# Block-sparse attention with a feed-forward layer: transposing P of the first 28 pairs on the tensor engine, and starting the feed-forward layer at slot 16

## The chip, the cores and the metric

The kernel runs on one core of a Trainium2 chip. The metric is device time in microseconds (us); lower is better. A core has a tensor engine (PE), a vector engine (DVE), a scalar engine (ACT), a GpSimd engine (POOL) and a sync engine (SP), each with its own in-order queue of instructions, and 16 DMA engines that all queues share.

## The reference

Attention over 4 batches, 8 heads, 768 positions, head size 64, with a mask by blocks of 32 positions: a block of queries sees its own block and its neighbours, the first and the last block, and three sampled blocks; the first and last query blocks see everything. Behind it stand a layer norm, a feed-forward layer (512 to 2048 to 512, ReLU) and a residual sum.

```python
scores = where(mask, q @ k.T / sqrt(D), -1e9)
attn   = softmax(scores)                    # per head, 768 x 768, block-sparse
x      = (attn @ v) -> (B, S, H * D)        # 4 x 768 x 512
xn     = (x - mean) / sqrt(var + 1e-6) * g_ln
out    = x + relu(xn @ w_ch1) @ w_ch2
```

Nearly every product is made of fp16 halves (a high part and a low part of each operand), so one product takes two or three matmuls.

## The kernel before

**Tiles, slots and pairs.** The rows of the output are 24 tiles of 128 query rows (two batches by two query blocks). 22 are sparse tiles with 8 x 32 keys each (kind "s"), and two, the 12th and the last, are dense ones ("d"). A tile has 8 heads; one head of one tile is a *slot*, so there are 192 slots, 0 to 191. In sparse tiles two heads are a *pair* (slots 2n and 2n+1 are pair n, until slot 87); softmax and the transpose of P are done once for a pair.

**The main loop** runs over slots `i`; for PE, SP and POOL its order is the program's order, while the order on DVE and ACT is set by the framework's scheduler. In slot `i` come, in this order: loads that an agenda has put there; the scores of slot `i` (16 matmuls in `scores`, tile `ps`, line 407, or 393 in a dense tile); after a pair's second slot its softmax (`softmax`: DVE takes the minimum, ACT makes exp into `e`, ACT casts the high half of `p`, DVE makes the low half, line 448); one slot later the transpose of `p` into `pt` (`transposes`, a DMA transpose of 256 KB issued by SP, line 459); and the product with V of slot `i - LAG`, LAG = 6 (`attn_v`, 16 matmuls into `pa`, line 481). After a tile's last head its layer norm follows (`layer_norm`), and when both tiles of a group of two have been normed, two slots later, their transposes (`ln_transposes`, 16 transposes on PE into `px`, line 516, two copies by ACT into `xT`, line 517).

**The feed-forward layer** (`ffn`) is a generator per group. It is stepped NFF = 24 times a slot from slot FF0 = 27 on. A slot's 24 steps are 24 up-projection matmuls of 256 columns (`pu`, line 533), whose 512 results per row ACT turns into `hh` (line 541) and DVE into `hl` (line 542); or 12 down-projection matmuls of 512 columns (`po`, line 552; each takes two steps). A group takes 8 slots of the first kind and 8 of the second, and a new group comes every 16 slots, so the layer keeps its distance behind the attention to the end. Behind each tile's down-projection stands the residual sum on DVE (line 558) and the store of `out`, issued by SP at once (line 560).

**Buffers.** `pu`, `po` and `px` take turns in one pool of three PSUM buffers (`ps_f`). `p` and `e` have two buffers each, `pt` three, the group's `xT`, `hh` and `hl` one each.

**Weights and K, V.** The weights come as 64-bit floats and are converted on the chip while attention runs: w1 in 8 pieces around slots 2 to 16, w2 in 16 pieces at slots 18 to 33 (a load on SP, three DVE operations, lines 224 to 228, ACT operations, lines 200 and 201 or 217 and 218, and a subtraction on POOL, line 203 or 220). K and V of the first two batches are split into halves before slot 0 and written to DRAM (`krow`, `vrow`; `write_k`, `first_v`, issued by SP); those of the other two from slot 50 on (`load_k`, slots 50 to 55; `load_v`, slots 57 to 62). A tile's K and V are read from there by SP (`kg`, `vg`) and gathered by POOL.

Of the kernel before, what the change touches and what calls it, by code (L numbers as in the profile page):

```python
# [44 lines left out]
def sparse_attention_moe(  # L45
# [26 lines left out]
    FF0 = 27  # L72
# [179 lines left out]
    def first_k(kr):  # L252
        kh, kl = (x[:, 0 : NB * H * BLK].rearrange("p (k e) -> p k e", k=NB) for x in k_f)
        for j in range(6):
# [4 lines left out]
            if j % 2:  # L259
                write_k(0, slice(4 * j - 4, 4 * j + 4), (kh, kl), slice(4 * j - 4, 4 * j + 4),  # L260
                        nc.sync)

    def first_v(vr):
        for b in range(2):
            for t in range(6):
# [4 lines left out]
                nc.sync.dma_start(vrow[0][t * P : (t + 1) * P, b, :],  # L270
                                  vs.rearrange("p h d -> p (h d)"))

    def write_k(f, bl, halves, src, dma):
# [236 lines left out]
    def ln_transposes(gr):  # L510
        gr.xT = lnp.tile([P, 2, CT, 2 * P], F16, tag="xT", name=f"xT{gr.i}")
        for j, t in enumerate(gr.tiles):
# [4 lines left out]
            nc.scalar.copy(gr.xT[:, :, :, j * P : (j + 1) * P], pt)  # L517


    def ffn(gr):  # L520
        N = 2 * P
        hh = hp.tile([P, FT, N], F16, tag="hh", name=f"hh{gr.i}")
        hl = hp.tile([P, FT, N], F16, tag="hl", name=f"hl{gr.i}")
        for f in range(0, FT, 2):
            ph = ps_f.tile([P, 512], F32, tag="pf", name=f"pu{gr.i}_{f}")
            while (1, f // 2) not in ready:
                yield
            for j in range(2):
                fs = slice((f + j) * P, (f + j + 1) * P)
                n = 0  # L530
                for w, i in ((w1h, 0), (w1l, 0), (w1h, 1)):
                    for ct in range(CT):
                        nc.tensor.matmul(ph[:, j * N : (j + 1) * N], w[:, ct, fs],  # L533
                                         gr.xT[:, i, ct, :], start=n == 0, stop=n == 3 * CT - 1,
                                         skip_group_check=True)
                        n += 1
                        if j == 0 or n < 3 * CT:
                            yield
            dh = hh[:, f : f + 2, :].rearrange("p f n -> p (f n)")
            dl = hl[:, f : f + 2, :].rearrange("p f n -> p (f n)")  # L540
# [208 lines left out]
```

## Time and profile before

| | |
|---|---|
| time, median of 3 runs | 905.37 us (904.17 to 906.74) |
| time of the profiled execution | 909.08 us |
| its span, first to last instruction | 907.2 us |
| mean granted clock of PE over the span | 0.906 of full speed |
| PE busy | 683.1 us (75%) |
| DVE busy | 466.8 us (51%) |
| ACT busy | 385.8 us (43%) |
| POOL busy | 314.3 us (35%) |

The profiled execution took 3.71 us more than the median, and 1.88 us of its time lie outside the span. A share of busy time is a mean over stages with different limits: PE is nearly always busy in the second half and mostly idle in the first quarter. So the views by stretch say more than this table.

### The profile page before, as it was taken

The page shows a single profiled execution, that of the slowest core. Times are in us where ns is not written, and L with a number is a line of the kernel's source. Part 1 is how long each engine was busy: PE and PEld are TensorE (multiplying, and loading weights), DVE is VectorE, ACT ScalarE, POOL GpSimd, SP SyncE. Part 2 cuts the span into 40 slices and gives each one's busy share as a digit, 9 for nine tenths or more (in the row PEclk, how much of TensorE's full clock was granted, in tenths as well). Part 3 has the DMA queues.
Part 4 walks back from the last instruction along what each step waited for, and adds up shares of the span by engine and source line. Part 5 has one row for each costly group of instructions (what it writes and reads, how often), then busy time and mean ns, then how long its engine had stood idle before and what let it go on. Part 6 is the DMA issues. An engine that isn't in the chain of part 4 may idle for free.

```text
span 907.2 us, 24132 instructions
## 1 busy us (share of the span) xinstructions
PE 683.1 (75%) x10304; PEld 446.9 (49%) x10304; DVE 466.8 (51%) x1144; ACT 385.8 (43%) x867; POOL 314.3 (35%) x284
## 2 busy tenths in 40 slices
PE   0011131548996767799987799999999999998998
PEld 0011121335583455366565376575856758466583
DVE  3638397577456443355573354455655546564120
ACT  3435364344454555344463244454444445543120
POOL 1247346435446766530060433343432331000000
PEclk9999555678998887799998799999999999999999
DMA  9999985939986979978999987878967697777000
GB/s 347 311 306 250 258 208 138 257 96 253 219 200 154 267 207 243 194 190 172 196 207 222 200 188 166 188 187 198 164 155 170 168 221 167 178 126 150 12 13 24
DMA packets 209226, 171.72 MB, mean 189 GB/s; under 512 B 151136, under 2 KB 176352, under 8 KB 208736
## 3 DMA queue, kind: packets, MB, share of 16 engines
q1 hardware_dynamic: 194064, 129.00, 61.5%
q0 software_dynamic: 13376, 40.91, 17.8%
q8 instruction: 81, 1.33, 0.7%
q10 hardware_dynamic: 1680, 0.28, 0.2%
q14 instruction: 25, 0.20, 0.1%
HBM read 121.91 MB, written 18.87 MB: 155 GB/s over the span
## 4 chain that ended last, share of the span: by engine, by line
PE 43%; DMA 26%; DVE 12%; ACT 8%; SPq 5%; issue 5%; POOL 0%; ACTq 0%; DVEq 0%; POOLq 0%
PE po L552 19%; PE pu L533 17%; DMA pt<-p 10%; DMA qr<-qT 7%; DMA vg<-vrow 3%; PE ps L407 3%; DVE p L448 3%; ACT e L443 3%; PE pa L481 3%; SPq L459 2%; ACT p L447 2%; DMA kr<-kT 2%; DVE e L436 2%; DVE st L440 1%; DVE hl L542 1%
## 5 line engine op out<-in xcount | busy, mean ns | idle before, releaser
L533 PE MATMUL pu<-xT,w1h 128*128 128x256 f16 x1536 | 224.8, 282 | 0.0
L481 PE MATMUL pa<-vg,pt 128*32 128x64 f16 (+1 forms) x3584 | 79.5, 217 | 133.4 <-DMA pt<-p 106.2
L340 POOL DMA_INDIRECT kg<-krow,ik x132 | 133.5, 1011 | 112.5 <-PE pa L481 42.4
L533 PEld LDWEIGHTS <-w1h 128*128 128x128 f16 x1536 | 148.0, 101 | 27.8
L448 DVE SCALAR_TENSOR_TENSOR p<-e,p 128x512 f16<-128x512 f32 (+1 forms) x104 | 92.6, 891 | 128.4 <-ACT p L447 128.1
L443 ACT ACTIVATE e<-e,st 128x256 f32<-128x256 f32 (+1 forms) x192 | 102.8, 536 | 126.1 <-DVE st L440 106.3
L552 PE MATMUL po<-w2h,hh 128*128 128x512 f16 x384 | 150.2, 391 | 0.4 <-DVE x L558 0.4
L552 PE MATMUL po<-w2l,hh 128*128 128x512 f16 x384 | 149.2, 389 | 0.0
L552 PE MATMUL po<-w2h,hl 128*128 128x512 f16 x384 | 149.1, 388 | 0.0
L313 POOL TENSOR_TENSOR ql<-qr,qx 64x1024 f16<-64x1024 f32 x24 | 51.0, 2124 | 236.8 <-ACT qx L312 236.7
L481 PEld LDWEIGHTS <-pt 128*32 128x32 f16 x3584 | 60.4, 102 | 141.9 <-DMA pt<-p 110.0
L533 PE MATMUL pu<-xT,w1l 128*128 128x256 f16 x768 | 121.6, 283 | 0.0
L552 PEld LDWEIGHTS <-hh 128*128 128x128 f16 x768 | 70.3, 100 | 81.2 <-issue 7.3
L436 DVE CUSTOM_DVE_ANT_1 e<-ps,bias 128x256 f32<-128x256 f32 x176 | 67.3, 418 | 67.4 <-PE ps L407 64.5
L407 PE MATMUL ps<-kg,qx 128*32 128x96 f16 (+1 forms) x1408 | 56.2, 236 | 52.1 <-DMA kg<-krow 44.7
L541 ACT ACTIVATE hh<-pu 128x512 f16<-128x512 f32 x96 | 56.4, 591 | 80.7 <-PE pu L533 80.3
L447 ACT CAST p<-e 128x512 f16<-128x512 f32 (+1 forms) x104 | 67.6, 650 | 53.2 <-DMA pt<-p 51.1
L533 PEld LDWEIGHTS <-w1l 128*128 128x128 f16 x768 | 78.1, 102 | 11.6
L542 DVE SCALAR_TENSOR_TENSOR hl<-pu,hh 128x512 f16<-128x512 f32 x96 | 65.8, 685 | 34.3 <-ACT hh L541 33.9
L407 PEld LDWEIGHTS <-qx 128*32 128x32 f16 x1408 | 25.1, 101 | 100.5 <-issue 98.6
L552 PEld LDWEIGHTS <-hl 128*128 128x128 f16 x384 | 38.4, 100 | 47.8 <-issue 4.1
L357 POOL DMA_INDIRECT vg<-vrow,iv x44 | 42.4, 963 | 47.4 <-PE pa L481 28.3
(82 smaller groups left out, 728.3 us busy)
## 6 DMA issues: line engine op xcount, KB each, us to landing
vg<-vrow SPq DMA_DIRECT2D x44, 384.0 KB, 6.3
qr<-qT SPq DMA_DIRECT2D x24, 512.0 KB, 8.2
kg<-krow SPq DMA_DIRECT2D x22, 512.0 KB, 6.9
w2r<-w SPq DMA_DIRECT2D x16, 512.0 KB, 5.7
out<-x SPq DMA_DIRECT2D x24, 256.0 KB, 3.0
kg<-krow SPq DMA_DIRECT2D x8, 768.0 KB, 9.9
vg<-vrow SPq DMA_DIRECT2D x8, 768.0 KB, 7.4
w2l<-w SPq DMA_DIRECT2D x4, 1024.0 KB
```

The source lines that it names most:

```text
L313: nc.gpsimd.tensor_sub(t.ql[0:D], qr[0:D], t.qx[0:D])
L340: nc.gpsimd.indirect_dma_start(t.k[:, 4 * j + 5 + r].rearrange("p b e -> p (b e)"), None, krow[t.f].rearrange("k p b e -> (k p) (b e)"), b ...
L407: nc.tensor.matmul(dst, q[:, h, rows], rhs, start=n == 0 and k == 0 and h % 2 == 0, stop=n == 1, skip_group_check=True)
L436: nc.vector.tensor_tensor_reduce(out=pr.e[:, k].rearrange("p (b k) -> p b k", k=BLK), in0=pr.ps[:, k], in1=bb, scale=-0.125, scalar=3.0e38 ...
L443: nc.scalar.activation(pr.e[:, k], pr.e[:, k], AF.Exp, bias=st[:, 1, h0 + k : h0 + k + 1], scale=-1.0, accum_out=st[:, 2, h0 + k : h0 + k ...
L447: nc.scalar.copy(pr.p[:, 0], e)
L448: nc.vector.scalar_tensor_tensor(out=pr.p[:, 1], in0=e, scalar=1.0, in1=pr.p[:, 0], op0=ALU.mult, op1=ALU.subtract)
L481: nc.tensor.matmul(t.xa[rows, h % 4, 0:w], pr.pT[:, i, k0 + k, rows], vv[:, k, 0:w], start=first and k == 0 and i == 0, stop=k == nk - 1 a ...
L533: nc.tensor.matmul(ph[:, j * N : (j + 1) * N], w[:, ct, fs], gr.xT[:, i, ct, :], start=n == 0, stop=n == 3 * CT - 1, skip_group_check=True)
L541: nc.scalar.activation(dh, ph, AF.Relu)
L542: nc.vector.scalar_tensor_tensor(out=dl, in0=ph, scalar=0.0, in1=dh, op0=ALU.max, op1=ALU.subtract)
L552: nc.tensor.matmul(po, x[:, f, ts], w[:, f, :], start=f == 0 and n == 0, stop=f == FT - 1 and n == 2)
```

## The change

Seven edits go together.

1. P of pairs 0 to 27 (slots 0 to 55) is no longer transposed by a DMA. `pe_transposes` does it in slot 2n + 4 for pair n (PELAG = 3 slots behind the pair's second slot): 8 transposes of 128 columns on PE into a buffer `pp` of the pool of three, and one copy of 128 x 1024 by ACT into `pt`. Pairs from 28 on keep the DMA transpose.
2. FF0 goes from 27 to 16. (NFF0 is 24 like NFF, so the steps per slot stay.)
3. The first group's layer-norm transposes are done tile by tile, two slots behind each tile's norm, that is in slots 15 and 23.
4. The first group's up-projection runs twice over the 8 pieces of w1, once per tile, with 128 columns instead of 256: slots 16 to 23 and 24 to 31. Its down-projection then takes slots 32 to 39, and group g (from 1 on) starts in slot 16g + 24 instead of 16g + 27.
5. The store of an output tile is issued at the start of a slot two slots behind the residual sum, not right behind it.
6. The high half of the first K is written to DRAM by ACT's queue and the low half by SP's.
7. The first V's 12 writes go to ACT's queue.

```diff
-    FF0 = 27
+    FF0 = 16
+    NFF0, FF0END = 24, 44
+    PEP, PELAG = 28, 3
...
                 write_k(0, slice(4 * j - 4, 4 * j + 4), (kh, kl), slice(4 * j - 4, 4 * j + 4),
-                        nc.sync)
+                        (nc.scalar, nc.sync))
...
-                nc.sync.dma_start(vrow[0][t * P : (t + 1) * P, b, :],
-                                  vs.rearrange("p h d -> p (h d)"))
+                nc.scalar.dma_start(vrow[0][t * P : (t + 1) * P, b, :],
+                                    vs.rearrange("p h d -> p (h d)"))
...
+    def pe_transposes(pr):
+        k = len(pr.heads) * 2
+        pr.pT = ptp.tile([P, 2, k, P], F16, tag="pt", name=f"pt{pr.i}")
+        pt = ps_f.tile([P, 2 * k, P], F16, tag="pf", name=f"pp{pr.i}")
+        p = pr.p.rearrange("p i k -> p (i k)")
+        for c in range(2 * k):
+            nc.tensor.transpose(pt[:, c], p[:, c * P : (c + 1) * P], ident)
+        nc.scalar.copy(pr.pT.rearrange("p i k q -> p (i k) q"), pt)
...
+        for lo, hi in ((0, 1), (1, 2)) if gr.i == 0 else ((0, 2),):
+            cs = slice(lo * P, hi * P)
+            N = (hi - lo) * P
+            for f in range(0, FT, 2):
+                ph = ps_f.tile([P, 512], F32, tag="pf", name=f"pu{gr.i}_{lo}_{f}")
+                while (1, f // 2) not in ready or gr.have < hi:
+                    yield
...
-            nc.sync.dma_start(out[t.i], x)
+            outq.append([2, t.i, x])
...
+            for o in outq:
+                o[0] -= 1
+            while outq and outq[0][0] <= 0:
+                _, n, x = outq.pop(0)
+                nc.sync.dma_start(out[n], x)
...
-                transposes(slots[i - 1].pr)
+                if slots[i - 1].pr.i >= PEP:
+                    transposes(slots[i - 1].pr)
+            if 0 <= i - PELAG < NS:
+                pr = slots[i - PELAG].pr
+                if pr.i < PEP and slots[i - PELAG] is pr.slots[-1]:
+                    pe_transposes(pr)
...
-                    if s.t.i % 2:
-                        lnq.append((i + 2, gr))
+                    if gr.i == 0:
+                        lnq.append((i + 2, gr, (s.t.i,)))
+                    elif s.t.i % 2:
+                        lnq.append((i + 2, gr, (0, 1)))
```

What it moves on the queues, at three places. First SP's queue between the start-up and slot 9, before (`vrow` are writes of the first V, `w2l` and `w2h` here loads of raw w1, `pt` transposes of P, `vg` loads of V):

```order
L350 DMA vg0_128<-vrow0_136 96x2048 x2
L270 DMA vrow0_136<-vs0_1_5_252 128x1024
L191 DMA w2l_125<-w1 128x4x512
L311 DMA qr1_328<-qT 128x1024
L459 DMA_TRANSPOSE pt0_350<-p0_316 128x8x128
L191 DMA w2l_125<-w1 128x4x512
L459 DMA_TRANSPOSE pt1_406<-p1_375 128x8x128
L191 DMA w2h_124<-w1 128x4x512
L328 DMA vg0_128<-vrow0_136 32x2048 x2
L459 DMA_TRANSPOSE pt2_461<-p2_432 128x8x128
L328 DMA vg1_129<-vrow0_136 32x2048 x4
L350 DMA vg1_129<-vrow0_136 96x2048 x2
```

and of the changed kernel:

```order
L352 DMA vg0_128<-vrow0_136 96x2048 x2
L193 DMA w2l_125<-w1 128x4x512
L313 DMA qr1_328<-qT 128x1024
L193 DMA w2l_125<-w1 128x4x512
L193 DMA w2h_124<-w1 128x4x512
L330 DMA vg1_129<-vrow0_136 32x2048
L330 DMA vg0_128<-vrow0_136 32x2048 x2
L330 DMA vg1_129<-vrow0_136 32x2048 x3
L352 DMA vg1_129<-vrow0_136 96x2048 x2
```

The three transposes and the write of V are gone from between the loads; in the rest of SP's queue the transposes of pairs 3 to 27 go in the same way.

Second ACT's queue around the first group's first copy of layer-norm transposes (`e` is the exponential, `p` the cast of P, `w2s`, `w2h` and `w1h` conversions of weights, `hh` a ReLU of the feed-forward layer), before:

```order
L200 ACTIVATE w2h_124<-w2h_124,g_sb_109 128x256 x4
L312 CAST qx3_1019<-qr3_1018 128x1024
L443 ACTIVATE e10_1187,st10_1186<-e10_1187,st10_1186 128x256 x2
L201 CAST w1h_122<-w2h_124 128x4x256
L217 ACTIVATE w2s0_1061<-w2s0_1061 128x512
L447 CAST p10_1193<-e10_1187 128x512
L499 ACTIVATE ls1_1215<-ls1_1215,eps_96 128x1
L217 ACTIVATE w2s1_1067<-w2s1_1067 128x512
L218 CAST w2h_124<-w2s0_1061 128x512
L517 COPY xT0_1328<-px0_1329 128x8x128
```

and of the changed kernel, where that copy stands three pairs earlier:

```order
L314 CAST qx3_1147<-qr3_1146 128x1024
L445 ACTIVATE e7_943,st6_828<-e7_943,st6_828 128x256 x2
L531 COPY xT0_970<-px0_971 128x8x128
L472 COPY pt6_1006<-pp6_1007 128x1024
L449 CAST p7_949<-e7_943 128x512
L202 ACTIVATE w2h_124<-w2h_124,g_sb_109 128x256 x4
L219 ACTIVATE w2s0_1225<-w2s0_1225 128x512
L219 ACTIVATE w2s1_1231<-w2s1_1231 128x512
L559 ACTIVATE hh0_1033<-pu0_0_0_1035 128x2x128
L203 CAST w1h_122<-w2h_124 128x4x256
```

Between a pair's exponential and its cast a copy of an earlier pair's transposed P now stands (`pt6` behind `e7`), and the first ReLU of 2 x 128 columns comes between the first pieces of w2.

Third PE's queue in slot 16 of the changed kernel (each kind of matmul with the weight load ahead of it, the last or the first of its run):

```order
L409 LDWEIGHTS ql0_130
L409 MATMUL ps16_989<-kg0_126,ql0_130 32x160
L471 LDWEIGHTS p6_835
L471 MATMUL pp6_1007<-ident_100,p6_835 128x128
...
L493 LDWEIGHTS pt5_893
L493 MATMUL pa1_0_905<-vg1_129,pt5_893 32x128
...
L551 LDWEIGHTS w1h_122
L551 MATMUL pu0_0_0_1035<-xT0_970,w1h_122 128x128
```

The 8 transposes of pair 6 stand between the scores of slot 16 and the product with V of slot 10, which uses pair 5; the up-projection with 128 columns follows in the same slot. Before, the product with V followed the scores directly, and no up-projection came until slot 27.

## Rows read from the trace of the kernel before

**Rows 1.** Busy time of each engine in eight stretches (columns: stretch in us, its length, then busy us of each engine with the number of instructions; granted clock of PE as a share of full speed; share of time that the 16 DMA engines were busy; GB/s). The bounds are the starts of slots 6, 16, 27, 40, 50 and 71, and of slot 191, the last.

```profile
core 0: us, PE busy (x) PEld busy (x) DVE busy (x) ACT busy (x) POOL busy (x), PEclk, DMA share, GB/s
0.00:55.36 55.36, 3.26 (x96) 2.70 (x96) 25.61 (x51) 20.64 (x30) 16.48 (x19) 1.00 0.96 324
55.36:111.30 55.94, 7.85 (x321) 6.70 (x325) 28.13 (x62) 25.12 (x61) 24.04 (x16) 0.79 1.09 265
111.30:160.25 48.95, 11.65 (x380) 9.19 (x372) 42.56 (x77) 24.20 (x58) 27.36 (x20) 0.50 0.74 181
160.25:237.07 76.82, 51.28 (x696) 33.81 (x684) 50.69 (x105) 35.89 (x80) 38.05 (x33) 0.80 0.82 193
237.07:269.32 32.25, 32.25 (x526) 23.43 (x526) 17.81 (x51) 14.73 (x39) 12.63 (x13) 1.00 0.93 215
269.32:381.43 112.11, 80.10 (x1049) 47.84 (x1048) 47.71 (x105) 50.26 (x106) 72.26 (x75) 0.82 0.88 218
381.43:816.96 435.53, 415.27 (x6418) 270.65 (x6417) 232.97 (x656) 199.06 (x470) 123.45 (x110) 0.97 0.84 183
816.96:907.20 90.24, 81.46 (x849) 52.57 (x848) 21.37 (x41) 15.89 (x27) 0.00 (x0) 0.98 0.21 49
```

**Rows 2.** The same stretches, instructions of line 407 alone (scores of sparse tiles; 16 matmuls are one slot), which is how the slots are counted.

```profile
55.36:111.30 55.94, 6.21 (x161) 4.34 (x165) 0.79 1.09 265
111.30:160.25 48.95, 7.05 (x176) 4.53 (x180) 0.50 0.74 181
160.25:237.07 76.82, 5.51 (x208) 3.14 (x208) 0.80 0.82 193
237.07:269.32 32.25, 4.07 (x161) 2.33 (x162) 1.00 0.93 215
269.32:381.43 112.11, 8.54 (x336) 4.87 (x336) 0.82 0.88 218
```

**Rows 3.** What PE waited for between slot 6 and slot 40: us in total, times, the longest.

```profile
PE pa L481 <- DMA pt<-p: 86.2, 13, 16.7
PE pa L481 <- DMA vg<-vrow: 12.3, 1, 12.3
PE px L516 <- DVE xl L507: 6.8, 1, 6.8
PE px L516 <- ACT xh L506: 4.5, 1, 4.5
```

**Rows 4.** Groups of DVE instructions in the same stretch (count, busy us, mean ns of one, idle time before them): the low half of a ReLU, 512 columns, and an operation of 256 columns that reads PSUM.

```profile
L542 DVE SCALAR_TENSOR_TENSOR hl<-pu,hh 128x512 f16<-128x512 f32 x8 | 5.5, 684 | 1.6 <-ACT hh L541 1.6
...
L488 DVE TENSOR_TENSOR x<-x,pa 128x256 f32<-128x256 f32 x8 | 3.3, 413 | 0.8 <-ACT x L487 0.8
```

**Rows 5.** ACT in the same stretch: the copy of layer-norm transposes.

```profile
L517 ACT COPY xT<-px 128x1024 f16<-128x1024 f16 x4 | 4.0, 1004 | 1.2 <-PE px L516 1.2
```

**Rows 6.** SP's queue in order of time, 17.5 to 82 us (start us, us, what it issues): the 12 writes of the first K, two transposes of P, and the load of V that stands behind them.

```profile
17.90 16.71 SPq L277 DMA_DIRECT2D krow<-kg  x12
...
58.27 2.11 SPq L459 DMA_TRANSPOSE pt<-p  x1
...
64.45 5.18 SPq L459 DMA_TRANSPOSE pt<-p  x1
...
70.38 0.98 SPq L328 DMA_DIRECT2D vg<-vrow  x2
```

**Rows 7.** PE in order of time around the layer-norm transposes of group 4: the first of four runs of 4 transposes, and the matmul behind the sixteenth.

```profile
434.38 0.40 PE L516 MATMUL px<-ident,xh 128*128 128x128 f16 x4
...
435.28 0.38 PE L552 MATMUL po<-w2h,hh 128*128 128x512 f16 x1
```

**Rows 8.** The chain of waits between 245 and 385 us (start us, us, what).

```profile
290.47 5.70 DMA kr<-kT
...
317.97 2.73 PE pu L533 x24
...
323.24 5.44 DMA pt<-p
...
337.27 5.54 DMA pt<-p
...
347.74 6.66 DMA pt<-p
...
357.81 17.91 DMA pt<-p
```

**Rows 9.** What PE waited for between 237 and 385 us.

```profile
PE pa L481 <- DMA pt<-p: 19.1, 4, 6.8
PE px L516 <- ACT xh L506: 11.3, 1, 11.3
```

**Rows 10.** DVE and ACT in order of time around the same transposes as in rows 7: the residual sum behind a down-projection, and the second copy into `xT`.

```profile
433.98 0.69 DVE L558 SCALAR_TENSOR_TENSOR x<-po,x 128x512 f32<-128x512 f32 x1 [0.20 <-PE po L552]
...
436.94 1.00 ACT L517 COPY xT<-px 128x1024 f16<-128x1024 f16 x1
```

**Rows 11.** The last pieces of the chain of waits, where PE does nothing but the last group: its 192 up-projection and the last 96 down-projection matmuls.

```profile
861.24 20.96 PE pu L533 x192
882.20 20.73 PE po L552 x96
```

**Rows 12.** The layer-norm transposes of the whole run on PE: count, busy us, mean ns of one.

```profile
L516 PE MATMUL px<-ident,xh 128*128 128x128 f16 x96 | 10.1, 231 | 17.5 <-ACT xh L506 17.5
```

More of the change, by code (lines that the diff above doesn't have):

```diff
@@ L276, in write_k @@
                 dst = krow[f][bl, half * D : (half + 1) * D, b, :]
-                dma.dma_start(dst.rearrange("k d e -> d k e"), x[b * D : (b + 1) * D, src])
+                dma[half].dma_start(dst.rearrange("k d e -> d k e"), x[b * D : (b + 1) * D, src])
     def load_k(f):
@@ L508, in layer_norm, with ln_transposes @@
                                        op0=ALU.mult, op1=ALU.subtract)
-    def ln_transposes(gr):
-        gr.xT = lnp.tile([P, 2, CT, 2 * P], F16, tag="xT", name=f"xT{gr.i}")
-        for j, t in enumerate(gr.tiles):
+    def ln_transposes(gr, js):
+        if js[0] == 0:
+            gr.xT = lnp.tile([P, 2, CT, 2 * P], F16, tag="xT", name=f"xT{gr.i}")
+        for j in js:
+            t = gr.tiles[j]
             pt = ps_f.tile([P, 2, CT, P], F16, tag="pf", name=f"px{t.i}")
@@ L517, in ln_transposes @@
             nc.scalar.copy(gr.xT[:, :, :, j * P : (j + 1) * P], pt)
+            gr.have = j + 1
     def ffn(gr):
[L521 to L526, printed above, removed]
-                yield
[L528 to L540, printed above, removed]
-            nc.scalar.activation(dh, ph, AF.Relu)
-            nc.vector.scalar_tensor_tensor(out=dl, in0=ph, scalar=0.0, in1=dh,
-                                           op0=ALU.max, op1=ALU.subtract)
-            yield
@@ new lines, in ffn @@
+        hh = hp.tile([P, FT, 2 * P], F16, tag="hh", name=f"hh{gr.i}")
+        hl = hp.tile([P, FT, 2 * P], F16, tag="hl", name=f"hl{gr.i}")
+        for lo, hi in ((0, 1), (1, 2)) if gr.i == 0 else ((0, 2),):
[5 more added lines that the diff above has]
+                    yield
+                for j in range(2):
+                    fs = slice((f + j) * P, (f + j + 1) * P)
+                    n = 0
+                    for w, i in ((w1h, 0), (w1l, 0), (w1h, 1)):
+                        for ct in range(CT):
+                            nc.tensor.matmul(ph[:, j * N : (j + 1) * N], w[:, ct, fs],
+                                             gr.xT[:, i, ct, cs], start=n == 0,
+                                             stop=n == 3 * CT - 1, skip_group_check=True)
+                            n += 1
+                            if j == 0 or n < 3 * CT:
+                                yield
+                dh, dl = hh[:, f : f + 2, cs], hl[:, f : f + 2, cs]
+                src = ph[:, 0 : 2 * N].rearrange("p (f n) -> p f n", f=2)
+                nc.scalar.activation(dh, src, AF.Relu)
+                nc.vector.scalar_tensor_tensor(out=dl, in0=src, scalar=0.0, in1=dh,
+                                               op0=ALU.max, op1=ALU.subtract)
+                yield
@@ L652, in sparse_attention_moe @@
                     layer_norm(s.t, gr, s.t.i % 2)
-                    if s.t.i % 2:
-                        lnq.append((i + 2, gr))
+                    if gr.i == 0:
+                        lnq.append((i + 2, gr, (s.t.i,)))
+                    elif s.t.i % 2:
+                        lnq.append((i + 2, gr, (0, 1)))
             if lnq and lnq[0][0] <= i:
-                gr = lnq.pop(0)[1]
-                ln_transposes(gr)
-                ffq.append(ffn(gr))
+                _, gr, js = lnq.pop(0)
+                ln_transposes(gr, js)
+                if js[0] == 0:
+                    ffq.append(ffn(gr))
             if i >= FF0:
-                for _ in range(NFF):
+                for _ in range(NFF0 if i < FF0END else NFF):
                     if ffq and next(ffq[0], "end") == "end":
```

6 lines of the change are left out of this document (3 added, 3 removed).

## The prediction

> **What bounds the kernel now.** I read the busy times by stretch first, then the same view of the score matmuls alone, which counts the slots, then PE's waits and the chain of waits. By the counts, the bounds in [rows 1] are the starts of slots 6, 16, 27, 40, 50 and 71 [rows 2]. The reader is to see four regimes. From slot 40 to 50 PE is never idle: 10 slots in 32.25 us, 3.23 us a slot, at full clock. From 381 us to the last slot it is busy 415.27 of 435.53 us. So these parts cost what their matmuls cost. From slot 6 to 40 (55.36 to 237.07 us, 181.7 us for 34 slots, 5.3 us a slot) PE is busy 70.8 us only, and 86.2 us of its idle time ended with a transposed P that landed, in 13 waits of up to 16.7 us [rows 3]. Its clock shows it: 0.50 between slots 16 and 27. From slot 50 to 71 (112.11 us for 21 slots, where 21 x 3.23 = 68 us would do) PE waits 11.3 us for a layer norm's high half and 19.1 us for P [rows 9]; in the chain four transposes of 5.44, 5.54, 6.66 and 17.91 us follow each other behind a load of K [rows 8].
>
> Behind the waits for P in slots 6 to 40, two other resources are not far off. DVE is busy 28.13 + 42.56 + 50.69 = 121.4 of 181.7 us, 67%, and 87% in the fullest stretch. The DMA engines have 1.09, 0.74 and 0.82 of 55.94, 48.95 and 76.82 us, together 160 us, 88% [rows 1]. So the time of this stretch cannot shrink by all of the 86.2 us.
>
> **Edits 1 to 4, slots 6 to 40.** All transposes of this stretch (pairs 0 to 18) move from SP's queue and the DMA engines to PE and ACT. PE's price: sixteen transposes start at 434.38 and the next matmul at 435.28, so 8 of them (fp16, 128 x 1024 to a pair) cost 0.45 us at full clock [rows 7] and at most 0.9 at half; 19 pairs make 9 to 17 us. The first group's up-projection now lies in slots 16 to 31, its down-projection in 32 to 39, in place of 27 to 42. That is PE time in a stretch where PE was idle 111 of 181.7 us, so both are hidden; without that cover the transposes would cost those 9 to 17 us. ACT pays one copy of 1.00 us a pair [rows 5], 19 us on top of its 85.2 of 181.7 us. DVE pays for 16 small halves instead of 8 full ones: 16 x 0.41 - 8 x 0.68 = 1.1 us, the small one taken at an operation of 256 columns from PSUM [rows 4]. So DVE's work is 122.5 us, and its share sets the length. If it stays at 67%, nothing is gained (182 us); at the 87% of the fullest stretch it is 141 us. I take 80%, 153 us, nearer the upper end, since most of PE's waits go, but not all of the way: ACT is then busy 104 of 153 us in one in-order queue with copies that wait for PE; two waits for layer norms (11.3 us) stay; and with 256 KB a transpose, at the 193 GB/s of the last stretch, the DMA engines lose 19 x 1.36 = 26 us and still have 134 of 153, 88% as now. The gain is 181.7 - 153.1 = **28.6 us** (0 to 41).
>
> **Edits 6 and 7, the start.** The writes of the first K hold SP's queue from 17.90 for 16.71 us; two transposes stand ahead of a load of V that is issued at 70.38 [rows 6]. That load is inside the stretch above; ahead of slot 6 the split of the writes gains at most some microseconds, because the DMA engines are busy 0.96 of the time. ACT takes over 18 writes: at SP's 16.71 / 12 = 1.4 us each at the most 25 us, covered by an ACT that is busy 20.64 of 55.36 us; uncovered they would delay the scores. I take **-2 us** (-6 to +3).
>
> **Slots 40 to 50.** PE is full here, so five pairs' transposes lie on the path: 5 x 0.45 = **+2.3 us**. P is ready long before: a pair's softmax has 2.5 slots, 8 us. ACT has room (14.73 of 32.25).
>
> **Slots 50 to 71.** Five more pairs, +2.3 us. Until pair 27 SP's queue holds no transpose, so the loads of the second K no longer stand behind one that waits for P, and ACT's cast of P no longer stands behind a K that lands late; that chain is what made the layer norm late (11.3 us of PE's wait). I take **-9 us** for it (0 to -13). The four waits in slots 62 to 70 are for pairs that keep the DMA transpose; they stay. POOL has 72.26 us of work here, so at 105 us it is at 69%; a gain much larger than 9 would have to pass it.
>
> **From slot 71.** The layer is three slots ahead to the end, so PE's last part without attention is three slots shorter: 20.96 / 8 = 2.62 us and 20.73 / 8 = 2.59 us a slot [rows 11], **-7.8 us**. Against it, a group's first up-projection now follows its layer-norm transposes by one slot. The second copy into `xT` ends at 437.94, 3.56 us behind the first transpose; the transposes (0.9), a slot's down-projection (2.6) and the next slot's scores and product with V (0.5, which is 3.23 less the 2.73 of a run of `pu` in [rows 8]) take 4.0 us, so it is just hidden. The buffer that it takes was the last down-projection's, whose residual sum takes 0.69 us [rows 10] against those 0.5: 0.25 us for each of 11 groups, **+2.7 us** (0 to +11, a copy one us late in every group). Edit 5 takes a wait for that sum out of SP's queue; SP's loads have slack there, and I count nothing (up to -4).
>
> **The sum.** -28.6 - 2 + 2.3 + 2.3 - 9 - 7.8 + 2.7 = -40.1 us against the profiled execution's 909.08: 869.0. The median of the runs is 3.7 us below it, so **865.3 us**.
>
> [...]
>
> **Rivals.**
> - *DVE runs nearly through* (chance 0.13). At 95% the stretch takes 129 us, 24 us less, for about **841 us**. For it: one stretch reaches 87% with waits in it. Against it: the DMA engines would have 134 us of work in 129.
> - *The DMA engines hold slots 6 to 40* (0.13). The stretch moves 265, 181 and 193 GB/s [rows 1], 38.5 MB, less 5.0 MB of transposes; if it goes on at 193 GB/s it takes 174 us, gains 8 and ends at **886 us**. For it: the weights of both layers must still come, and DVE already waits for them. Against it: the first row shows 265 GB/s with transposes among them.
> - *The three shared PSUM buffers and ACT's queue couple PE to ACT* (0.15). Transposes, up- and down-projection and layer-norm transposes take turns in three buffers; a late ReLU or copy stops PE, which delays the next scores. DVE's share rises to 71% (172.5 us, gain 9), and the wait at slot 55 stays: **894 us**. For it: `pt6` stands behind `px0` on ACT, which waits for a layer norm. Against it: ACT would be busy 60%.
> - *A transpose costs its full latency* (0.03). At 231 ns each [rows 12], unpipelined, a pair takes 1.85 us and the ten pairs on the path 18.5 instead of 4.6: **879 us**.
> - *Slower* (0.05). `pe_transposes` stands in PE's in-order queue two slots ahead of where P was needed; scores, product with V and up-projection queue behind it, and DVE and ACT wait for those scores. Once each of the 28 pairs holds PE up by 40.1 / 28 = 1.4 us more than I expect, the gain is gone; at 1.8 us it is about **915 us**. For it: the copy and the cast share ACT with the loads of the second K. Against it: from slot 40 to 50 nothing makes P late.
> - *The wait only passes on* (0.03): PE then waits for the loads of V (12.3 us now, [rows 3]) as long as for P, and the layer-norm and buffer costs eat the three slots: **905 us**.
>
> **How the numbers follow.** My forecast has 0.48, with its own range from 850 to 879: the share of DVE between 76 and 87%, the other terms partly with it. The range for 8 in 10 runs from 842 to 892: it leaves out the slower and the unchanged case, half of the coupled one's upper side, and the fastest half of the first rival. About 0.3% (2.7 us) is what a measurement can tell from no change. All cases but the last two are faster: 0.92; unchanged 0.03; slower 0.05.
>
> **What would show it.** Right: no wait of PE for `pt` before slot 62; 80 us less idle time of PE before slot 40, with DVE's share near 80% and slot 40 at about 206 us; PE's clock at 1.00 well before 227 us; slot 55 without its wait; the part behind the last attention 8 us shorter. Wrong: long waits of `pp` for `p` or of PE for an ACT copy; DVE's share still below 72%; or up-projections that wait for `xT` or the residual sum by more than 0.5 us in every group.

## The result

The changed kernel takes 865.48 us (median of 4 runs, 860.5 to 874.47), the kernel before 904.77 on the same chip (4 runs, 901.4 to 906.74): 0.955 of the time before, 95% interval 0.948 to 0.962. The ratio leaves out the slowest run of the changed kernel, which is more than 1.5% above its fastest; the two medians as they stand give 0.957. The forecast was 865.3 us.

The profiled execution of the changed kernel is its fastest, 860.5 us with a span of 858.6. Against the profiled execution of before that is 48.6 us less, while the medians differ by 39.3. Where one term hangs on that difference, the third experiment serves as a second sample of nearly the same kernel.

Busy time by stretch, the bounds again the starts of slots 6, 16, 27, 40, 50, 71 and 191, to be held beside [rows 1] (columns as there):

```profile
0.00:58.10 58.10, 4.37 (x106) 3.37 (x108) 27.61 (x60) 23.61 (x41) 17.27 (x19) 1.00 0.98 333
58.10:112.43 54.33, 15.06 (x376) 11.35 (x369) 39.45 (x67) 30.23 (x64) 30.61 (x20) 0.76 0.95 292
112.43:160.12 47.69, 32.93 (x675) 28.51 (x674) 39.88 (x80) 32.65 (x77) 29.05 (x24) 0.74 0.54 175
160.12:220.93 60.81, 46.23 (x698) 26.20 (x697) 39.98 (x95) 34.92 (x77) 29.19 (x25) 0.89 0.54 158
220.93:256.54 35.61, 35.61 (x578) 26.91 (x578) 19.51 (x53) 21.36 (x44) 14.94 (x15) 1.00 0.50 152
256.54:346.44 89.90, 75.83 (x1078) 45.42 (x1078) 48.30 (x105) 53.03 (x109) 70.35 (x74) 0.96 0.87 239
346.44:775.90 429.46, 411.33 (x6457) 272.69 (x6457) 232.58 (x658) 198.93 (x472) 122.03 (x110) 0.98 0.87 186
775.90:858.60 82.70, 73.77 (x777) 45.58 (x776) 19.79 (x39) 14.61 (x25) 0.00 (x0) 0.97 0.22 55
```

The gain has three places. Slots 6 to 40 take 162.8 us instead of 181.7. Of these 18.9 us 16.0 come behind slot 27 (60.8 instead of 76.8); the 2.9 ahead of it only make up for the later start, and slot 27 begins at 160.1 us where it began at 160.25. Slots 50 to 71 take 89.9 instead of 112.1. From slot 71 on it is 6.1 us less in the long stretch and 7.5 in the part behind the last attention. Slots 40 to 50 are 3.4 us longer, the start 2.7.

What PE waited for between slots 6 and 40, to be held beside [rows 3], the six longest (us in total, times, the longest):

```profile
PE pa L493 <- DMA vg<-vrow: 18.4, 1, 18.4
PE pp L471 <- DVE p L450: 10.9, 6, 2.5
PE pu L551 <- DVE hl L560: 8.6, 2, 6.6
PE pp L471 <- ACT p L449: 7.4, 4, 3.2
PE px L530 <- ACT xh L518: 7.0, 1, 7.0
PE po L570 <- POOL w2l L222: 5.9, 2, 3.9
```

The 86.2 us for a transposed P are gone. In their place stand 18.3 us in which the transposes wait for P itself, and 23.9 us of other waits for DVE and POOL, against 8.7 before. The longest single wait is the one for V in slot 6, 18.4 us against 12.3. The same view between slots 50 and 71 (in [rows 9] a wait of 11.3 us for `xh` and 19.1 us for `pt`; that window began at slot 40, where nothing waited):

```profile
PE pa L493 <- DMA pt<-p: 8.6, 3, 3.8
PE pa L493 <- ACT pt L472: 2.9, 1, 2.9
PE px L530 <- ACT xh L518: 1.9, 1, 1.9
```

### The profile page after: what moved, and what is told of

The parts are those of the page before. It is cut to its first block, busy times and chain, and to the rows that moved or that the text cites. A ratio compares the mean times of both kernels' runs of the same rounds, so it can differ in the third digit from the quotient of the medians.

```text
span 858.6 us, 24902 instructions
## 1 busy us (share of the span) xinstructions
PE 695.1 (81%) x10720; PEld 460.0 (54%) x10720; DVE 467.1 (54%) x1152; ACT 409.3 (48%) x903; POOL 313.4 (37%) x284
## 4 chain that ended last, share of the span: by engine, by line
PE 56%; DMA 19%; DVE 9%; POOL 5%; issue 5%; ACT 4%; SPq 1%; ACTq 0%; POOLq 0%; DVEq 0%
PE po L570 23%; PE pu L551 23%; DMA pt<-p 6%; DMA qr<-qT 5%; PE ps L409 4%; PE pa L493 3%; DMA vg<-vrow 2%; DVE p L450 2%; POOL kg L342 1%; PE px L530 1%; DMA krow<-kg 1%; DMA krow<-kh 1%; DMA vrow<-vs 1%; DVE w2s L228 1%; DVE x L501 1%
## 5 line engine op out<-in xcount | busy, mean ns | idle before, releaser
L551 PE MATMUL pu<-xT,w1h 128*128 128x256 f16 (+1 forms) x1664 | 223.1, 269 | 9.9 <-DVE hl L560 8.6
L342 POOL DMA_INDIRECT kg<-krow,ik x132 | 131.2, 994 | 111.2 <-issue 31.4
L551 PEld LDWEIGHTS <-w1h 128*128 128x128 f16 x1664 | 150.3, 100 | 32.5 <-issue 7.7
L450 DVE SCALAR_TENSOR_TENSOR p<-e,p 128x512 f16<-128x512 f32 (+1 forms) x104 | 88.5, 851 | 72.7 <-ACT p L449 72.4
L438 DVE CUSTOM_DVE_ANT_1 e<-ps,bias 128x256 f32<-128x256 f32 x176 | 67.4, 419 | 103.4 <-PE ps L409 100.4
L551 PE MATMUL pu<-xT,w1l 128*128 128x256 f16 (+1 forms) x832 | 120.6, 269 | 0.0
L493 PE MATMUL pa<-vg,pt 128*32 128x128 f16 (+1 forms) x3584 | 77.5, 215 | 46.5 <-DMA vg<-vrow 27.7
L493 PEld LDWEIGHTS <-pt 128*32 128x32 f16 x3584 | 58.0, 101 | 56.4 <-issue 36.8
L560 DVE SCALAR_TENSOR_TENSOR hl<-pu,hh 128x512 f16<-128x512 f32 (+1 forms) x104 | 67.0, 644 | 38.6 <-ACT hh L559 38.5
L559 ACT ACTIVATE hh<-pu 128x512 f16<-128x512 f32 (+1 forms) x104 | 57.5, 557 | 51.2 <-PE pu L551 50.9
L570 PEld LDWEIGHTS <-hl 128*128 128x128 f16 x384 | 38.5, 100 | 54.3 <-issue 11.2
```

The source lines that it names most:

```text
L342: nc.gpsimd.indirect_dma_start(t.k[:, 4 * j + 5 + r].rearrange("p b e -> p (b e)"), None, krow[t.f].rearrange("k p b e -> (k p) (b e)"), b ...
L438: nc.vector.tensor_tensor_reduce(out=pr.e[:, k].rearrange("p (b k) -> p b k", k=BLK), in0=pr.ps[:, k], in1=bb, scale=-0.125, scalar=3.0e38 ...
L450: nc.vector.scalar_tensor_tensor(out=pr.p[:, 1], in0=e, scalar=1.0, in1=pr.p[:, 0], op0=ALU.mult, op1=ALU.subtract)
L493: nc.tensor.matmul(t.xa[rows, h % 4, 0:w], pr.pT[:, i, k0 + k, rows], vv[:, k, 0:w], start=first and k == 0 and i == 0, stop=k == nk - 1 a ...
L551: nc.tensor.matmul(ph[:, j * N : (j + 1) * N], w[:, ct, fs], gr.xT[:, i, ct, cs], start=n == 0, stop=n == 3 * CT - 1, skip_group_check=True)
L559: nc.scalar.activation(dh, src, AF.Relu)
```

## The experiments

Theories. **A**: DVE's busy time sets slots 6 to 40, by a share that it can reach. **B**: what sets them is that POOL's subtractions hold up DVE's operations, and that other engines then wait for these. **C**: loads do (the DMA engines, or the load of V in slot 6). The expectations letter their theories anew for each run; there a letter means what stands behind it. Beside them stands the question which of the seven edits earns the time.

Twelve runs were made on three chips. On the first the kernel before takes 904.5 us, on the others 985.07 and 984.92. So runs are compared on one chip, or by their ratio to the kernel before, which stands with its 95% interval in brackets.

### Transposes on PE alone

```diff
# before, with edit 1 only
+    PEP, PELAG = 28, 3
...
-                transposes(slots[i - 1].pr)
+                if slots[i - 1].pr.i >= PEP:
+                    transposes(slots[i - 1].pr)
... # pe_transposes and its call in the loop, as in the change
```

> The kernel before with edit 1 alone (P of pairs 0 to 27 on PE; the feed-forward layer from slot 27 as before). Theory A, the transposes give the gain between slot 50 and slot 71 (112 us before, 90 in the changed kernel), because SP's queue no longer holds a transpose between the loads of the second K: about 90 us there, and slot 40 at 215 to 225 us as in the changed kernel; in all 872 to 882 us. Rival B, the layer that starts early and the store that is issued late give the gain from slot 50 on: 105 to 112 us between slots 50 and 71, in all 890 us or more.

Measured: 882.05 us (5 runs, 879.24 to 889.61), ratio 0.974 [0.969, 0.979]. Slots 6 to 40, 40 to 50, 50 to 71, 71 to 191 and the rest:

```profile
58.30:218.00 159.70, 86.51 (x1523) 60.19 (x1511) 117.82 (x234) 96.96 (x207) 91.02 (x70) 0.68 0.68 208
218.00:253.60 35.60, 35.60 (x569) 25.73 (x572) 16.64 (x47) 19.49 (x40) 13.08 (x12) 1.00 0.58 172
253.60:350.00 96.40, 81.77 (x1093) 49.15 (x1096) 51.91 (x109) 54.08 (x111) 70.25 (x74) 0.90 0.84 221
350.00:793.10 443.10, 413.01 (x6421) 269.31 (x6420) 230.80 (x654) 197.41 (x469) 122.74 (x110) 0.98 0.84 180
793.10:887.60 94.50, 84.48 (x849) 53.99 (x848) 22.74 (x43) 16.29 (x29) 0.00 (x0) 0.94 0.19 48
```

The whole early gain is here: 159.7 us for slots 6 to 40, less even than the 162.8 of the full change. PE is idle in 73.2 of them without a single wait for a DMA's transpose. 15.7 of the 22.2 us of slots 50 to 71 are here too. Behind slot 71 nothing is gained: the profile has 7.6 and 4.3 us more there than the one of before, but it is of an execution that took 7.6 us more than the median of the five. Slots 50 to 71 came out between theory A (90 us) and its rival (105 or more), nearer A.

The DMA engines' busy time in slots 6 to 40 falls from 160 us (0.88 of 181.7) to 109 (0.68 of 159.7), with 19 DMA transposes gone. By an estimate from these figures a transpose took 2.7 us of all 16 engines, twice the 1.36 that the prediction took from its bytes.

### The layer early alone

```diff
# changed kernel, without edits 1, 5, 6, 7
-    PEP, PELAG = 28, 3
+    PEP, PELAG = 0, 3
...
-            outq.append([2, t.i, x])
+            nc.sync.dma_start(out[t.i], x)
... # both halves of the first K and the first V written by nc.sync again
```

> The kernel before with edits 2 to 4 alone (the layer from slot 16, the first group tile by tile with 128 columns; all transposes of P by DMA, stores and start as before). Theory A: the part behind the last attention is 8 us shorter, the stretches ahead of slot 71 stay within 6 us of before (slot 40 at 235 us, slots 50 to 71 in 108 to 114 us), in all 893 to 899 us. Rival B: 875 to 885 us, with slots 50 to 71 in 95 us or less.

Measured: 898.91 us (10 runs, 892.87 to 904.77), ratio 0.994 [0.990, 0.999]. The same first stretch and the last:

```profile
54.20:235.50 181.30, 83.90 (x1618) 58.56 (x1610) 116.83 (x249) 87.09 (x207) 91.58 (x69) 0.88 0.86 218
815.00:900.90 85.90, 75.49 (x777) 46.07 (x776) 20.10 (x39) 14.50 (x25) 0.00 (x0) 0.96 0.22 51
```

This is theory A. Early PE work does not shorten slots 6 to 40 (181.3 against 181.7) while P comes by DMA: PE's clock rises from 0.72 to 0.88 and nothing ends sooner. What it earns is at the end, where 777 matmuls stand instead of 849 and take 85.9 us instead of 90.2.

### The start undone

```diff
# changed kernel
-                        (nc.scalar, nc.sync))
+                        (nc.sync, nc.sync))
...
-                nc.scalar.dma_start(vrow[0][t * P : (t + 1) * P, b, :],
+                nc.sync.dma_start(vrow[0][t * P : (t + 1) * P, b, :],
```

> The changed kernel without edits 6 and 7 (the first K and V are written from SP's queue). Theory A: the two edits are worth nothing, since slot 6 starts at 58 us in the changed kernel and at 55 before: within 3 us of the changed kernel, slot 6 at 55 to 59 us. Rival: the writes on ACT's queue bring the loads of V forward behind it, and without them PE's wait at slot 6 (18.4 us in the changed kernel) grows by 5 us or more, in all 5 us or more slower than the changed kernel.

Measured: 866.08 us (4 runs, 863.79 to 867.82), ratio 0.957 [0.951, 0.962]: edits 6 and 7 are worth nothing that can be measured. Slot 6 starts at 58.0 us here, 58.1 in the changed kernel and 58.3 with the transposes alone, but at 54.2 with the layer alone and 55.4 before. So the 2.7 us lost at the start belong to the transposes, which stand in PE's queue from slot 4 on and wait for the first P.

### The store at once

```diff
# changed kernel
-            outq.append([2, t.i, x])
+            nc.sync.dma_start(out[t.i], x)
```

> The changed kernel without edit 5 (the store of an output tile is issued right behind its residual sum). My prediction counted nothing for it; from slot 71 on the changed kernel is 13.6 us shorter than before where 5.1 was forecast. Theory A (the rest is fewer waits for loads behind a store that waits): the part from slot 71 is 3 to 8 us longer than in the changed kernel, in all 3 to 8 us slower. Rival: the store has no part in it, within 2 us of the changed kernel.

Measured: 877.72 us (4 runs, 872.36 to 879.83), ratio 0.969 [0.963, 0.975], 11.6 us above the third experiment on the same chip. So the delayed store, for which the sum had nothing, is worth more than any edit but the transposes. Theory A (3 to 8 us) was too low, and its rival (within 2) is out. What SP's queue waited for from slot 71 on, first with the delayed store (the third experiment, L663), then with the store at once (L578), one row of each:

```profile
SPq L663 <- DVE x L576: 58.0, 4, 30.9
```

```profile
SPq L578 <- DVE x L576: 116.5, 15, 31.0
```

And busy time from slot 71 to 191 and behind it, the third experiment ahead of this one:

```profile
355.30:784.20 428.90, 411.02 (x6453) 272.05 (x6452) 233.09 (x657) 198.99 (x472) 122.53 (x110) 0.98 0.85 184
784.20:865.60 81.40, 72.23 (x777) 44.58 (x776) 19.92 (x39) 14.50 (x25) 0.00 (x0) 1.00 0.23 55
```

```profile
354.60:790.20 435.60, 412.61 (x6457) 272.65 (x6457) 234.97 (x659) 199.52 (x473) 121.91 (x110) 0.98 0.87 184
790.20:876.30 86.10, 76.67 (x777) 46.32 (x776) 20.10 (x39) 14.50 (x25) 0.00 (x0) 0.94 0.22 53
```

With the store at once SP stops 15 times for a residual sum, 116.5 us in all, and what stands behind that store in its queue stops with it. Of the 6.7 us between the two long stretches 5.1 are idle time of PE (22.99 against 17.88): its waits for loads of V grow from 11.9 to 14.6 us, those for layer norms and a ReLU from 0.5 to 4.8. How SP's stops lead to these waits is argued and not shown: SP's waits together are as long in both runs (340 and 339 us), because it waits less for P with the store at once (154.8 us against 225.9). The other 4.7 us, behind the last attention, go with a granted clock of 0.94 against 1.00; what lowered the clock there the runs do not show.

Beside the kernel before, the transposes alone gain 22.5 us and the layer early alone 5.6; the store gains 11.6 and the start nothing. Together that is 39.7 us, and the change as a whole gains 39.3.

### More pairs on PE, and two ways to lighten DVE

Second chip.

```diff
# e5_pep36 and e8_pep44: changed kernel
-    PEP, PELAG = 28, 3
+    PEP, PELAG = 36, 3        # 44 in e8
# e6_less_dve: changed kernel, one of DVE's three conversions of a weight left out
-        nc.vector.scalar_tensor_tensor(out=wf, in0=raw[:, :, 0], scalar=29, in1=wf,
-                                       op0=ALU.logical_shift_right, op1=ALU.bitwise_or)
# e7_pool_writes_only: changed kernel
-        nc.gpsimd.tensor_sub(w1l[:, :, fs], src, w1h[:, :, fs])
+        nc.gpsimd.memset(w1l[:, :, fs], 0.0)
...
-        nc.gpsimd.tensor_sub(w2l[:, i, :], src, w2h[:, i, :])
+        nc.gpsimd.memset(w2l[:, i, :], 0.0)
```

> The changed kernel with P of 36 pairs transposed on PE instead of 28 (slots 56 to 71 too). The waits of PE for a DMA transpose in slots 60 to 70 (8.6 us between 221 and 350 us in the changed kernel, and 27 us of transposes in the chain there) are the last of their kind. Theory A, they go: slots 50 to 71 take 80 to 84 us instead of 90, eight more transposed pairs cost 8 x 0.67 = 5.4 us of PE, in all 3 to 8 us faster than the changed kernel. Rival, POOL sets that stretch (70.35 of 89.9 us busy): it stays at 88 to 92 us and the kernel is equal or some us slower.

> The changed kernel with P of 44 pairs transposed on PE (all sparse tiles ahead of the first dense one, slots 0 to 87). Behind slot 71 PE is full, and the changed kernel waits there for a DMA transpose only 2 us. Theory A: against 36 pairs this costs 8 x 0.67 = 5.4 us more, less what the smaller load on SP's queue gives back (0 to 3 us). Rival: SP's queue has become the limit of the loads, and 44 pairs are faster than 36 by 3 us or more.

> The changed kernel without the third DVE operation of every weight conversion (the lowest three bits of each weight's mantissa stay out, so the output is a little off). That takes 16 x 0.75 + 6 x 1.22 = 19 us of DVE's 119 out of slots 6 to 40. Theory A (DVE's work sets this stretch, as in my prediction): it shrinks by 19 us or more from 163, to 144 or less. Rival B (DVE waits in a chain with ACT, POOL and PE, and its work is only a part of the chain): by 4 to 12 us. Rival C (loads set it): by less than 4 us.

> The changed kernel with POOL writing zeros for the low halves of the weights instead of subtracting (these terms of the products are left out, so the output is a little off). In slots 6 to 40 some DVE operations take up to 6.7 us instead of 0.4, while POOL subtracts; together DVE is held up by about 27 us there. Theory P (POOL's subtractions hold DVE up): the held-up time falls below 15 us and the stretch shrinks by 8 us or more. Rival (the time is hidden by other waits): the held-up time falls, the stretch stays within 5 us of 163.

Measured, with the length of slots 6 to 40 in the profile: 36 pairs 955.2 us (4 runs, 950.98 to 963.89), 164.0; 44 pairs 958.71 (4 runs, 958.58 to 959.55), 165.9; less DVE work 940.86 (2 runs), 159.2; POOL writing only 935.0 (2 runs, 930.49 and 939.5), 150.3. Against the two runs with more pairs, to leave out a third of DVE's conversions takes 5 to 7 us out of the stretch (rival B of that run, 4 to 12), and to take the reads out of POOL's subtractions takes 14 to 16 (theory P, 8 or more). That speaks for B. 44 pairs stand 3.5 us above 36, as theory A had it (2.4 to 5.4), but the runs overlap. But the changed kernel itself had not run on this chip, so it was run next, with a version that moves the work instead of leaving it out.

### Low halves on DVE, beside the changed kernel

Third chip.

```diff
# e9_changed_again: the changed kernel. e11 is e7 and e12 is e5 once more.
# e10_low_halves_on_dve: changed kernel
-        nc.gpsimd.tensor_sub(w1l[:, :, fs], src, w1h[:, :, fs])
+        nc.vector.tensor_sub(w1l[:, :, fs], src, w1h[:, :, fs])
...
-        nc.gpsimd.tensor_sub(w2l[:, i, :], src, w2h[:, i, :])
+        nc.vector.tensor_sub(w2l[:, i, :], src, w2h[:, i, :])
```

> The changed kernel itself, unedited, beside the next three on one chip, so that the pair (36 transposes on PE, less work for DVE, POOL writing only), which so far stands beside no run of it on its own chip, can be judged. Every theory expects the ratio to the kernel before that the first timing showed, 0.955 (0.948 to 0.962), and 160 to 166 us for slots 6 to 40.

> The 24 low halves of the weights that POOL subtracts in slots 6 to 40 (and the rest of them) are subtracted by DVE. DVE's own work grows by about 16 x 0.68 + 8 x 1.2 = 20 us (the 0.68 of a DVE operation that reads 128 x 512 fp32 and writes fp16, the 1.2 of one of 128 x 1024), and the time for which POOL's subtractions held DVE's operations up (27.6 us over their usual duration in these slots) shrinks by about as much. Theory A (DVE's busy time with the hold in it sets slots 6 to 40): no gain, 163 us, +-5, and the same total, 860 to 870. Theory B (what costs time is single DVE operations held for 2 to 7 us while PE, ACT or a load wait for them, and POOL's low halves that come late): 150 to 156 us, total 7 to 13 us less than the changed kernel. Theory C (DVE's own work, hold or not): 170 to 180 us, total 10 us more.

> POOL only writes zeros where it subtracts the low halves of the weights, so the low halves are missing from the result; repeated beside the changed kernel. Theory A and B (DVE held up by POOL's subtractions): 148 to 153 us for slots 6 to 40 against 160 to 166 of the changed kernel, and a total about 10 us less. If the 150.3 us of the first such run belonged to its chip: as the changed kernel, within 3 us.

> 36 pairs instead of 28 transposed on PE, beside the changed kernel. If the loads of P for pairs 28 to 35 were what PE waits for in slots 50 to 71 (8.6 us in three waits): 8.6 less, plus eight pairs at 0.67 us: 3 us less in all. If these transposes only add work to a PE that is the bound: 5 us more. The first such run stood at 0.974 of the kernel before, against 0.955 of the changed kernel on another chip: if that is the effect of the edit and not of the chip, 17 us more.

Measured: changed kernel 951.93 us (950.02 to 955.37), ratio 0.967 [0.959, 0.974]; low halves on DVE 942.44 (941.33 to 943.35), 0.956 [0.949, 0.963]; POOL writing only 934.86 (929.95 to 940.23), 0.947 [0.940, 0.954]; 36 pairs 954.65 (947.22 to 957.56), 0.970 [0.962, 0.977]; 4 runs each. Slots 6 to 40 of the changed kernel, of the one with the low halves on DVE, and of the one in which POOL only writes:

```profile
58.60:226.60 168.00, 98.09 (x1748) 68.83 (x1737) 115.47 (x239) 97.39 (x212) 89.20 (x68) 0.81 0.66 200
```

```profile
61.90:213.70 151.80, 93.17 (x1748) 65.64 (x1742) 113.51 (x261) 96.18 (x212) 53.89 (x44) 0.82 0.72 214
```

```profile
61.10:205.80 144.70, 93.82 (x1748) 67.37 (x1736) 101.05 (x239) 95.87 (x211) 67.35 (x68) 0.83 0.74 227
```

The changed kernel itself missed what was expected of it (0.948 to 0.962, and 160 to 166 us). DVE does 22 operations more and is busy 2.0 us less, and the stretch is 16.2 us shorter, as B had it (150 to 156, 7 to 13 us in all; 9.5 measured). A falls, since DVE's busy time hardly changed and the stretch did; so does C of this run's expectation, by which DVE's own work would have made it 170 to 180. With POOL writing only, the gain is larger than expected, 17.1 us in all (about 10) with 144.7 us for the stretch (148 to 153).

Loads (C of the list above) are ruled out only behind slot 16, where all of the gain lies: 7.6 us up to slot 27 and 9.4 behind it, with no transfer taken away. Slots 6 to 16 take 55.9 us with the low halves on POOL and 56.6 with them on DVE; the DMA engines are busy 0.94 and 0.93 of that time, and PE waits 18.7 and 16.2 us for V. There C is open. Of the 16.2 us the total keeps 9.5: slot 6 starts 3.2 us later with the low halves on DVE, and slots 71 to 191 take 502.8 us instead of 496.7; the runs do not show why. The rows of the operations concerned, in the same stretch, first of the changed kernel, where POOL subtracts, then with the low halves on DVE:

```profile
L501 DVE TENSOR_TENSOR x<-x,st 128x256 f32<-128x256 f32 x8 | 10.3, 1290 | 0.1
L222 POOL TENSOR_TENSOR w2l<-w2s,w2h 128x512 f16<-128x512 f32 x16 | 20.2, 1265 | 27.8 <-ACT w2h L220 27.7
L205 POOL TENSOR_TENSOR w1l<-w2h,w1h 128x1024 f16<-128x1024 f32 x8 | 18.2, 2275 | 8.7 <-ACT w1h L203 8.7
```

```profile
L501 DVE TENSOR_TENSOR x<-x,st 128x256 f32<-128x256 f32 x8 | 3.3, 415 | 0.0
L222 DVE TENSOR_TENSOR w2l<-w2s,w2h 128x512 f16<-128x512 f32 x16 | 10.8, 685 | 6.3 <-ACT w2h L220 5.8 <-ACT e L445 0.5
L205 DVE TENSOR_TENSOR w1l<-w2h,w1h 128x1024 f16<-128x1024 f32 x6 | 7.3, 1215 | 1.7 <-ACT w1h L203 1.7
```

DVE subtracts in about half of POOL's time, and its own `x` operation falls from 1290 to 415 ns. Summed over the stretch, DVE's operations exceed the median time of their kind by 24.2 us in the changed kernel and by 6.4 with the low halves on DVE. The 17.8 us between them make room for the 18.1 us of subtractions. Not told apart is how much of the 16 us comes from the hold and how much from POOL's queue, in which gathers of K and V no longer stand behind 28 us of waits for ACT: this edit takes away both. The run in which POOL only writes takes away both as well.

36 pairs are as good as 28 (2.7 us more, between the 3 less and the 5 more of the expectation; the runs overlap), and the 17 us that the first such run seemed to cost were its chip. The version with the low halves on DVE beats both kernels.

## Why the prediction came out right, term by term

The total was right to 0.2 us, but the terms behind it were not: what slots 6 to 40 fell short of the forecast was made up behind slot 50. That it came so close is luck: the interval of the measurement alone is 6 us to either side, and in the profile misses of +9.7 us (slots 6 to 40) and +4.7 (the start) stand against -15.5 and -8.8 (slots 50 to 71, and 71 to 191). In us against before, by the spans of the profiles:

| term | forecast | profile | third experiment |
|---|---|---|---|
| start | -2 | +2.7 | +2.6 |
| slots 6 to 40 | -28.6 | -18.9 | -15.5 |
| slots 40 to 50 | +2.3 | +3.4 | +3.4 |
| slots 50 to 71 | -6.7 | -22.2 | -16.6 |
| slots 71 to 191 | +2.7 | -6.1 | -6.6 |
| behind the last attention | -7.8 | -7.5 | -8.9 |
| sum | -40.1 | -48.6 | -41.6 |

**The start.** The step that failed is the 2 us that the two edits were to gain. Undone, they change nothing, and the transposes cost what the start lost: PE waits 2.7 us for the first P ahead of slot 6.

**Slots 6 to 40.** The step that failed is DVE's share of 80%. It is 119.3 of 162.8 us, 73%, and slot 40 starts at 220.9 us, not 206; PE is idle 68.6 us instead of 110.9, 42 less and not 80. The view that was read for it, busy time, cannot show the cause: part of DVE's busy time is time held up. Where POOL subtracts, one DVE operation of 0.4 us shows as 6.72 us. DVE and POOL at 123 us of the changed kernel (start, duration):

```profile
123.03 0.42 DVE L500 TENSOR_TENSOR x<-x,pa 128x256 f32<-128x256 f32 x1 [1.82 <-ACT x L499]
123.48 6.72 DVE L501 TENSOR_TENSOR x<-x,st 128x256 f32<-128x256 f32 x1
123.50 2.13 POOL L205 TENSOR_TENSOR w1l<-w2h,w1h 128x1024 f16<-128x1024 f32 x1
125.59 2.12 POOL L315 TENSOR_TENSOR ql<-qr,qx 64x1024 f16<-64x1024 f32 x1
127.67 2.25 POOL L222 TENSOR_TENSOR w2l<-w2s,w2h 128x512 f16<-128x512 f32 x2
130.13 0.41 DVE L560 SCALAR_TENSOR_TENSOR hl<-pu,hh 128x256 f16<-128x256 f32 x1
```

The low half `hl` that ends this stretch is the one that PE waited 6.6 us for (the third row of PE's waits above). PE waits there for a buffer of the pool of three to be read, so the prediction's third rival, the shared buffers, has its part in these slots too: 162.8 us lie half-way between the forecast's 153.1 and that rival's 172.5. Of the signs of being wrong one came in part: `pp` waits for `p` by 18.3 us, in ten waits of at most 3.2. With the low halves on DVE 151.8 us were reached, a share of 75%: the forecast's 153 us was a length that this stretch can have, but not with this change.

**The layer early in slots 6 to 40.** That PE's work hides there was right; but the first group's layer-norm transposes, now done tile by tile, stand in PE's queue from slot 15 on and wait there for the layer norm. Slots 6 to 16 take 45.1 us with the transposes alone (58.3 to 103.4), without such a wait, and 54.3 in the changed kernel; two waits make 9.1 us of that difference:

```profile
PE px L530 <- ACT xh L518: 7.0, 1, 7.0
PE px L530 <- DVE xl L519: 2.1, 1, 2.1
```

Up to slot 40 `px` waits 16.4 us where the prediction let 11.3 stay. Slots 16 to 40 are shorter with the layer early (108.5 us against 114.6), and the stretch as a whole ends about even (162.8 and 159.7).

**Slots 40 to 50.** PE is full there and the clock is 1.00, as said. A pair costs 0.67 us and not 0.45. PE and its neighbours in slot 40 of the changed kernel:

```profile
220.93 0.29 PE L409 MATMUL ps<-kg,qx 128*32 128x96 f16 x8
221.27 0.62 PE L471 MATMUL pp<-ident,p 128*128 128x128 f16 x8
221.82 0.35 PE L493 MATMUL pa<-vg,pt 128*32 128x128 f16 x16
224.83 0.29 PE L409 MATMUL ps<-kg,qx 128*32 128x96 f16 x8
```

From the first transpose to the next matmul it is 0.55 us, and the slot takes 3.90 us where one without transposes takes 3.23. Over the ten slots the clock is 1.00 with 40 transposes among 578 matmuls; a stretch of transposes alone was not run.

**Slots 50 to 71.** That no P transposed by a DMA is waited for before slot 62 was right (the first such wait is in slot 64); the P of slot 60, transposed on PE, is waited for by 2.9 us, until ACT has copied it. The step that failed is that the waits behind it stay: they belong to pairs that keep the DMA transpose, but fall from 19.1 to 8.6 us, and the one for `xh` from 11.3 to 1.9. PE waits 19.9 us less for these two, against 9 in the sum, and the 2.9 us for ACT's copy are new; slot 55 keeps 2.2 us; the clock rises from 0.82 to 0.96 and PE's busy time falls from 80.10 to 75.83 us, which the sum had not counted. In the third experiment the wait for P fell less, to 14.1 us, and the stretch is 95.5 us long.

**From slot 71.** The part behind the last attention came out as forecast (-7.5, 72 matmuls fewer), but not for the three slots alone: the two runs with the layer early and the store at once have the same 777 matmuls there and gain only 4.3 and 4.1 us (85.9 and 86.1). The rest goes with the delayed store or with the clock, which differs between these runs (0.96 and 0.94, against 0.97); that was not told apart. The charge for the shared buffers was wrong in full (and its own sum gives 11 x 0.19 = 2.1 us, not 2.7): PE waits for `xT` by 1.2 us in the whole run and nowhere for a residual sum.

```profile
PE pu L551 <- ACT xT L531: 1.2, 2, 0.9
```

The delayed store was priced at nothing, with up to 4 us in the range, because SP's loads seemed to have slack. In the kernel before SP's queue waits at its store 21 times, and taking the edit back costs 11.6 us. The row is of the kernel before, over its whole span:

```profile
SPq L560 <- DVE x L558: 104.3, 21, 31.0
```

What was missed is what the prediction did for P in slots 50 to 71: to ask which loads stand behind a waiting instruction.

## What to carry to other kernels

When a wait of 86 us goes, ask what it had covered: here 42 us came back from PE's idle time, the rest went to waits for other engines. Busy time does not tell work from waiting inside an instruction (here 0.42 us showed as 6.72): compare one operation's duration with its usual one before a share of it is made into a bound, and try to move work off an engine whose instructions hold up others: here 24 subtractions given to the fuller engine shortened the stretch by 16.2 us. And a store that waits for a result belongs behind the loads in an in-order queue: here, issued two slots later, it was worth 11.6 us.

## What the runs showed of the hardware

**Some DVE operations stop while POOL subtracts.** In the timeline above one DVE operation was held through four POOL operations in a row (the last of their rows stands for two), 6.30 us over its usual 0.42. The same happened in the kernel before, to an operation on 128 x 2 elements, 6.74 us where its median over the run is 0.16:

```profile
140.14 6.74 DVE L440 TENSOR_SCALAR st<-st 128x2 f32<-128x2 f32 x1
140.44 2.13 POOL L203 TENSOR_TENSOR w1l<-w2h,w1h 128x1024 f16<-128x1024 f32 x1
```

By their recorded starts both DVE operations began ahead of POOL's, by 0.02 and 0.30 us. The `x` operation has both its inputs in SBUF, the one on 128 x 2 elements has one tensor as its input. Four operations `hl`, with one input in PSUM, ran beside POOL's subtractions in slots 6 to 40 of the changed kernel, 0.41 to 0.42 us each, and none was held. What decides it the runs do not show. One of the four:

```profile
159.47 1.17 POOL L222 TENSOR_TENSOR w2l<-w2s,w2h 128x512 f16<-128x512 f32 x1
159.62 0.42 DVE L560 SCALAR_TENSOR_TENSOR hl<-pu,hh 128x256 f16<-128x256 f32 x1 [1.09 <-ACT hh L559]
```

**Three chips, two speeds.** The kernel before takes 904.5 us on one chip and 985 on two others. PE's waits from 365 to 860 us of the changed kernel on the third chip, the two longest:

```profile
PE pa L493 <- issue: 23.2, 36, 1.2
PE pu L551 <- issue: 9.8, 16, 1.2
```

On the first chip there is no such wait in this stretch. Most of them come in every eighth slot (72, 104 to 144, 160 and 168), which takes 8 to 10 us there while most others take 3.2 to 4.1, at gaps of 0.5 or 1.2 us between matmuls that wait for nothing in the profile; the clock of the stretch is 0.92 instead of 0.98. The cause is open. The gain of the change there is 33.0 us instead of 39.3.
